# Up products of a SwiGLU block in row halves of the array: two of 64 rows side by side instead of one of 128

## The chip, the core and the metric

The kernel runs on one core of a Trainium2 chip. The metric is the device time of one execution in microseconds (us): 907.65 us is the median of three runs of the kernel before (907.55 to 908.18). The core has a matrix engine (TensorE; PE in the profile, with its weight loads listed apart as PEld), a vector engine (DVE), an activation engine (ACT), GpSimd (POOL) and SyncE (SP), the last two here mainly for starting DMA transfers. TensorE reads both operands from SBUF and writes to PSUM, which here is handed out as four tiles of two banks; one bank holds 512 fp32 values in each of 128 partitions.

## The reference

Hash attention on four batches of eight heads, and then a SwiGLU feed-forward block over all 3,072 rows of its output:

```python
scores = scale * np.matmul(q, k.transpose(0, 1, 3, 2))
scores = np.where(mask, scores, -1000000000.0)       # mask: q and k fall into the same bucket
...
x = attn_out.transpose(0, 2, 1, 3).reshape(B * S, H * D)      # 3072 x 512
g = x @ w_gate                                                # 512 x 1536
silu = g * (1.0 / (1.0 + np.exp(-g)))
val = x @ w_val
return (silu * val @ w_out).astype(np.float32)
```

The change concerns only `x @ w_gate` and `x @ w_val`, the "up" products.

## The kernel before, in words

**Two stages.** Attention comes first (0 to about 314 us of the profile), then the feed-forward block (314 us to the end), in `gated_block`. The order of work on every engine is written out by hand: instructions run on each engine in the order in which the program issues them.

**Split values.** The feed-forward block multiplies in the one-pass fp32 form of TensorE (`FP32R`). For accuracy each operand is kept in three parts: a high part h (index 0), a low part l (index 1) and their difference d (index 2). A product needs one accumulator for h and l together, called `a`, and one for the differences, called `n`. The result is `a` times a constant minus `n`.

**Tiling.** The 3,072 rows of x are taken in three blocks of 1,024 (`WB`), the 1,536 columns of the weights in twelve pieces `f` of 128. x lies transposed, so that its 512 columns are the contraction: four slices j of 128 (`NJ` = 4). For one piece F and one of "gate" and "value", the function `up` makes one up product: 128 columns of the weights by 1,024 rows of x, accumulated over four slices j. PSUM tile `a` gets 16 matrix instructions of 128 contraction rows and 512 columns (4 slices x 2 parts x 2 halves of the 1,024), and tile `n` gets 8 (4 slices x 1 part x 2 halves). The two halves lie in two different banks of the tile. There are 3 x 12 x 2 = 72 up products, so 1,152 instructions into `a` and 576 into `n`.

**Order around them.** In `atoms_of`, an up product has two atoms. The atom `one` issues `first` (all into `a`) and has ACT copy `a` out of PSUM, scaled (line 787). The atom `other` issues `second` (all into `n`); then DVE subtracts `n` (line 794). For the gate, ACT applies Silu (line 796). For the value, DVE multiplies with the gate (line 798), and ACT and DVE split the result into three parts, `hid` (lines 799, 805 and 808). After each three pieces f a "down" product D follows: eight chunks of nine instructions (128 rows, 512 columns) into PSUM tiles `o`, which read `hid` and w_out. In each block the order is U0 to U3, D0, U4 to U6, D1, U7 to U9, D2, U10, U11, D3, where each U is a gate and a value up product. In D3 the first four chunks begin with the two older of their three `hid` pieces, since the third is still being made.

**Row halves elsewhere.** In attention, the score products (line 549, tile `sc`) already use 64 contraction rows each: the head in partitions 0 to 63 writes one bank of its tile and the head in partitions 64 to 127 the other. The products with v (line 580, tile `av`) use 64 output columns, the row sums and hashes (tile `joint`) 32.

**Weights.** Each up product reads one ring tile of 768 KB, brought from DRAM by POOL (`bring`, line 251), six tiles in all. A ring tile comes free when the last instruction of `second` has read it.

Of the kernel before, what the change touches and what calls it, by code (L numbers as in the profile page):

```python
# [19 lines left out]
def kernel(  # L20
# [20 lines left out]
    nc = tc.nc  # L41
# [3 lines left out]
    P = 128  # L45
# [7 lines left out]
    NJ = DM // P  # L53
    NF = DF // P
    PIECE = 512
    NQ = 3
    assert DF % P == 0 and DM == PIECE and NF % NQ == 0
    WB = 2 * PIECE
    NB = B * S // WB
    assert NB * WB == B * S and S < WB < 2 * S and NF // NQ > 2  # L60
    assert 2 * D == P and S == NCH * P and NCH % 2 == 0 and HQ <= 512 and DM <= 512
# [19 lines left out]
    def two_banks(name):  # L81
        return pp.tile([P, 2, 512], FP32, tag="pp", name=name)
# [3 lines left out]
    def r32(t):  # L86
        return t.bitcast(FP32R)
# [8 lines left out]
    for f in range(NF):  # L96
        for src in (moe_w_gate, moe_w_val):
            pieces.append(src.rearrange("(j p) c -> p j c", p=P)[:, :, 2 * f * P : 2 * (f + 1) * P])
        if f % NQ == 0 and f or f == NF - 1:
            done = (f + 1) // NQ * NQ if f == NF - 1 else f  # L100
            for g in range(done - NQ, done):
                pieces.append(moe_w_out[g * P : (g + 1) * P, :])
    place = {}
    n = 0
    for f in range(NF):
        place["g", f], place["v", f] = n, n + 1
        n += 2
        if f % NQ == 0 and f or f == NF - 1:
            done = (f + 1) // NQ * NQ if f == NF - 1 else f
# [3 lines left out]
    NPIECE = len(pieces)  # L113
    ram = [dram.tile([P, 3, PIECE], FP32R, tag=f"ram{i}", name="ram") for i in range(NPIECE)]
    words = {}
# [7 lines left out]
    def load_words(count, queue=None):  # L123
        queue = queue or queues[0]
        for i in range(len(words), min(count, NPIECE)):
            words[i] = t = wordp.tile([P, PIECE, 2], I32, tag="words", name="words")
            to = t.rearrange("p f w -> p (f w)")
# [4 lines left out]
    def scale(i):  # L132
        t = words[i]
        if i // 2 not in stages:
            stages[i // 2] = stagep.tile([P, 2, 3, PIECE], FP32, tag="stage", name="stage")
        staged[i] = st = stages[i // 2][:, i % 2]
# [104 lines left out]
    def bring(count=1):  # L241
        for _ in range(count):
# [6 lines left out]
            pool = ringp[2 <= i % sum(RINGS) < 2 + RINGS[1]]  # L249
            held[what, n] = t = pool.tile([P, 3, PIECE], FP32R, tag="ring", name="ring")  # L250
            nc.gpsimd.dma_start(t.bitcast(FP32), ram[at].bitcast(FP32))  # L251
# [3 lines left out]
    xparts = {}  # L255
# [480 lines left out]
    def gated_block(scope):  # L736
# [2 lines left out]
        hidp = scope.enter_context(tc.tile_pool(name="hidp", bufs=4))  # L739
        outp = scope.enter_context(tc.tile_pool(name="outp", bufs=1))  # L740
        homes.append(outp)
        hids = {}
        accs = {}
        rows = [out[b * S : (b + 1) * S, :].rearrange("(p c) m -> p c m", c=NCH) for b in range(B)]
        NCB = WB // P

        def mm(ps, w, x, start, stop):
            nc.tensor.matmul(ps, w, x, start=start, stop=stop)  # L748

        def up(F, what):  # L750
            b = F // NF
            w = held[what, F]
            a, n_ = two_banks("a"), two_banks("n")

            def block(v, j):
                return w[:, v, j * P : (j + 1) * P]

            def first():
                for j in range(NJ):
                    for v in range(2):  # L760
                        for half in range(WB // PIECE):
                            mm(a[:, half], block(v, j), r32(xparts[b, j][:, half, v]),
                               j == 0 and v == 0, j == NJ - 1 and v == 1)

            def second():
                for j in range(NJ):
                    for half in range(WB // PIECE):
                        mm(n_[:, half], block(2, j), r32(xparts[b, j][:, half, 2]),
                           j == 0, j == NJ - 1)

            return first, second, a, n_

# [3 lines left out]
        def atoms_of(kind, n):  # L776
            if kind == "U":
# [5 lines left out]
                for what, z in (("g", gate), ("v", val)):  # L783
                    def one(what=what, z=z):
                        ops[what] = up(n, what)
                        ops[what][0]()
                        nc.scalar.activation(two(z), ops[what][2], AF.Copy, scale=STEP + 1)  # L787
# [27 lines left out]
            else:  # L815
# [5 lines left out]
                def start(c, js, steps=None):  # L821
                    if c not in tiles:
                        tiles[c] = two_banks("o")
                    t = tiles[c]
                    cols = slice(c * P, (c + 1) * P)
                    def first():
                        for j in js:
                            for v in range(2):
                                mm(t[:, 0], hs[j][:, v, cols], ws[j][:, v],
                                   j == 0 and v == 0, j == NQ - 1 and v == 1)  # L830

                    def second():
                        for j in js:
                            mm(t[:, 1], hs[j][:, 2, cols], ws[j][:, 2], j == 0, j == NQ - 1)

                    for go in steps or ("ba" if final and c >= ahead else "ab"):
                        (first if go == "a" else second)()
# [93 lines left out]
        for kind, n in order:  # L931
            b, f = divmod(n, NF if kind == "U" else NF // NQ)
# [43 lines left out]
    with ExitStack() as scope:  # L976
        gated_block(scope)
# [32 lines left out]
```

## Time and profile before

| what | value |
|---|---|
| median of three runs | 907.65 us |
| the profiled execution, its own time | 908.05 us |
| its span, first to last instruction | 906.3 us |
| TensorE busy | 901.8 us of the span |
| DVE, ACT, POOL busy | 665.4, 450.4, 90.6 us |
| instructions into `a`, `n`, `o` | 1152, 576, 870 |
| their busy time | 273.0, 142.2, 198.2 us |
| granted TensorE clock, mean | 0.999 |

How to read it: the profile lists groups of instructions by source line, engine and tiles, as "out<-in", with the array tile (rows*columns), the shape, the number, the busy time and the mean length of one. A matrix instruction's length includes the time in which its last columns pass through the array, during which the next one already runs, so lengths overlap. What a stream of them costs is read from the distance between starts. Times are microseconds from the start of the span unless marked ns.

### The profile page before, as it was taken

To read this page: it belongs to the slowest core of one execution; us is meant where nothing else is said; L and a number is where in the kernel's file an instruction comes from. 1 tells how busy PE (TensorE), PEld (TensorE's weight loads), DVE (VectorE), ACT (ScalarE), POOL (GpSimd) and SP (SyncE) were. 2 spreads that over 40 slices of the span, in tenths; PEclk is the share of its full clock that TensorE was granted. 3 is DMA by queue.
4 is the path that set the end of the run, shared out by engine and by line. 5 is a ranking of instruction groups with operands and counts; after the bars stand their busy time and mean duration, and the time that the engine had idled before them with its cause. 6 is when DMAs were issued, how large, how long until landed. Compare 5 with 4: busy or idle time off the path is not lost.

```text
span 906.3 us, 12438 instructions
## 1 busy us (share of the span) xinstructions
PE 901.8 (100%) x4801; PEld 638.4 (70%) x4801; DVE 665.4 (73%) x782; ACT 450.4 (50%) x604; POOL 90.6 (10%) x187
## 2 busy tenths in 40 slices
PE   9999999999999999999999999999999999999998
PEld 5444444444444588888888888888888888888887
DVE  6779999999988977688786856464658754474746
ACT  6788988788888654551524233331313243413220
POOL 2001100010001210011000000101000100001000
PEclk9999999999999999999999999999999999999999
DMA  7567888877877799685758563534434642525332
GB/s 181 109 145 183 190 203 194 205 203 230 229 195 213 225 358 375 240 294 170 300 173 296 193 249 105 180 134 172 142 140 150 250 149 98 200 70 209 104 140 93
DMA packets 142266, 174.24 MB, mean 192 GB/s; under 512 B 103200, under 2 KB 113408, under 8 KB 142208
## 3 DMA queue, kind: packets, MB, share of 16 engines
q0 software_dynamic: 22240, 114.83, 35.8%
q1 hardware_dynamic: 118560, 57.43, 24.5%
q10 hardware_dynamic: 1408, 1.20, 0.5%
q8 instruction: 38, 0.62, 0.3%
q14 instruction: 20, 0.16, 0.1%
HBM read 133.17 MB, written 39.42 MB: 190 GB/s over the span
## 4 chain that ended last, share of the span: by engine, by line
PE 99%; DVE 0%; DVEq 0%; issue 0%
PE a L748 29%; PE o L748 21%; PE sc L549 17%; PE n L748 14%; PE av L580 14%; PE joint L621 1%; PE joint L441 1%; PE idle L375 0%; PE tps L483 0%; DVE o L843 0%; DVE o L851 0%; DVE o L886 0%; DVEq L1005 0%; DVE kb L369 0%
## 5 line engine op out<-in xcount | busy, mean ns | idle before, releaser
L748 PE MATMUL a<-xparts,ring 128*128 128x512 f32 x1152 | 273.0, 389 | 0.0
L748 PEld LDWEIGHTS a<-xparts,ring 128*128 128x128 f32 x1152 | 216.2, 188 | 45.4 <-issue 0.6
L748 PE MATMUL o<-ring,hid 128*128 128x512 f32 (+1 forms) x870 | 198.2, 388 | 0.0
L748 PEld LDWEIGHTS o<-ring,hid 128*128 128x128 f32 x870 | 162.9, 188 | 33.6
L559 ACT ACTIVATE A<-sc 128x768 f32<-128x768 f32 x192 | 154.0, 815 | 1.6 <-PE sc L549 0.8
L549 PE MATMUL sc<-qT,kT 64*128 64x384 f32 x768 | 153.0, 483 | 0.0
L748 PE MATMUL n<-xparts,ring 128*128 128x512 f32 x576 | 142.2, 389 | 0.0
L580 PE MATMUL av<-A,vraw 128*64 128x386 f32 (+1 forms) x768 | 127.7, 488 | 0.0
L748 PEld LDWEIGHTS n<-xparts,ring 128*128 128x128 f32 x576 | 108.1, 188 | 22.4
L794 DVE TENSOR_TENSOR v<-v,n 128x1024 f32<-128x1024 f32 x36 | 44.0, 1221 | 97.5 <-PE n L748 97.0
L251 POOL DMA_DIRECT2D ring<-ram x108 | 57.0, 530 | 498.7 <-PE n L748 302.4
L580 PEld LDWEIGHTS av<-A,vraw 128*64 128x64 f32 x768 | 53.7, 136 | 73.3 <-issue 62.6
L787 ACT ACTIVATE g<-a 128x1024 f32<-128x1024 f32 x36 | 37.0, 1027 | 128.0 <-PE a L748 126.9
L549 PEld LDWEIGHTS sc<-qT,kT 64*128 64x128 f32 x768 | 68.8, 187 | 39.8 <-issue 35.3
L799 ACT ACTIVATE hid<-v 128x1024 fp32r<-128x1024 f32 x36 | 38.2, 1062 | 111.9 <-DVE v L798 108.2
L796 ACT ACTIVATE g<-g 128x1024 f32<-128x1024 f32 x36 | 38.2, 1061 | 87.9 <-DVE g L794 87.9
L855 DVE TENSOR_TENSOR o<-o 128x512 f32<-128x512 f32 x92 | 62.9, 687 | 19.0 <-ACT o L849 16.6
L794 DVE TENSOR_TENSOR g<-g,n 128x1024 f32<-128x1024 f32 x36 | 43.8, 1217 | 37.5 <-PE n L748 37.5
L549 PE MATMUL sc<-qb,kb 64*128 64x384 bf16 x384 | 63.5, 323 | 0.0
L603 DVE SCALAR_TENSOR_TENSOR both<-A 128x1536 f32<-128x1536 f32 x32 | 55.5, 1734 | 4.5 <-ACT A L559 3.0
L805 DVE SCALAR_TENSOR_TENSOR hid<-hid,v 128x1024 fp32r<-128x1024 f32 (+1 forms) x39 | 44.5, 1141 | 18.8 <-ACT hid L799 18.8
L607 DVE TENSOR_TENSOR both<-both,A 128x1536 f32<-128x1536 f32 x32 | 55.9, 1748 | 1.7
(88 smaller groups left out, 695.5 us busy)
## 6 DMA issues: line engine op xcount, KB each, us to landing
ring<-ram POOLq DMA_DIRECT2D x108, 768.0 KB, 5.6
ram<-stage POOLq DMA_DIRECT2D x22, 768.0 KB, 4.5
ram<-stage SPq DMA_DIRECT2D x14, 768.0 KB
vraw<-in_v_dram SPq DMA_DIRECT2D x16, 384.0 KB
kraw<-in_k_dram SPq DMA_DIRECT2D x60, 96.0 KB
qraw<-in_q_dram SPq DMA_DIRECT2D x60, 96.0 KB
r<-sums SPq DMA_DIRECT2D x28, 192.0 KB
out_dram<-o SPq DMA_DIRECT2D x10, 512.0 KB
```

Source lines behind the costliest of these rows:

```text
L251: nc.gpsimd.dma_start(t.bitcast(FP32), ram[at].bitcast(FP32))
L549: nc.tensor.matmul(banks_of[u][:, h], x["k", n][rows, ks], x["q", n][rows, qs], start=start, stop=stop)
L559: nc.scalar.activation(weights(u)[:, :, 0:HQ], banks_of.pop(u), AF.Exp, scale=SCALE * (1.0 if units[u][0] else OFF / 2))
L580: nc.tensor.matmul(ps[h * D : (h + 1) * D, 0:width], raws["v", n][:, h, c, :], a[:, h, 0:width], start=c == 0, stop=c == NCH - 1)
L603: nc.vector.scalar_tensor_tensor(out=t, in0=first, scalar=S * EPS / P / 2, in1=now, op0=ALU.add, op1=ALU.add)
L607: nc.vector.tensor_tensor(t, t, now, op=ALU.add)
L748: nc.tensor.matmul(ps, w, x, start=start, stop=stop)
L794: nc.vector.tensor_tensor(two(z), two(z), n_, op=ALU.subtract)
L796: nc.scalar.activation(z, z, AF.Silu)
L799: nc.scalar.activation(h, val, AF.Copy, scale=TOWARD / STEP)
L805: nc.vector.scalar_tensor_tensor(out=l_, in0=h_.bitcast(FP32), scalar=-STEP, in1=v_, op0=ALU.mult, op1=ALU.add)
L855: nc.vector.tensor_tensor(accs[c], accs[c], t[:, 1], op=ALU.subtract)
```

## The change

An up product's 24 instructions of 128 contraction rows become 48 of 64. They are issued in pairs: one takes partitions 0 to 63 of a slice j and a part v and writes one half of the 1,024 columns, and the other takes partitions 64 to 127 and writes the other half, in the other bank. After one pass over all slices each half has had only half of the contraction. A second pass, with `swap` = 1, gives each half the other 64 partitions. The passes follow one another as: `a`, `n`, `a` swapped (all three in `first`), `n` swapped (in `second`). An added helper `after` puts a dependency between the last instruction of a tile's first pass and the first of its second pass, so that TensorE waits there for its own earlier instruction. In the list of each engine's instructions, nothing but TensorE's is different; DVE, ACT, POOL and SP have the same instructions in the same order.

```diff
+    HALF = P // 2
...
+        def after(later, earlier):
+            with tc.tile_pool(name="turn", bufs=1) as pool:
+                tc.add_manual_dep(pool.alloc_inst, earlier.ins.name, sync, reason="turn")
+                tc.add_manual_dep(later.ins, pool.alloc_inst.name, sync, reason="turn")
...
+            def rows_of(out, v, j, half, at, start, stop):
+                rows = slice(at * HALF, (at + 1) * HALF)
+                return mm(out[:, half], w[rows, v, j * P : (j + 1) * P], r32(xparts[b, j][rows, half, v]),
+                   start, stop)
+
+            ends = {}
+
+            def turn_of(out, vs, swap):
+                for j in range(NJ):
+                    for v in vs:
+                        for at in range(2):
+                            first_, last_ = j == 0 and v == vs[0], j == NJ - 1 and v == vs[-1]
+                            i = rows_of(out, v, j, at ^ swap, at, not swap and first_, bool(swap) and last_)
+                            if at == 0 and first_ and swap:
+                                after(i, ends[vs])
+                            if last_:
+                                ends[vs] = i
+
             def first():
-                for j in range(NJ):
-                    for v in range(2):
-                        for half in range(WB // PIECE):
-                            mm(a[:, half], block(v, j), r32(xparts[b, j][:, half, v]),
-                               j == 0 and v == 0, j == NJ - 1 and v == 1)
+                turn_of(a, (0, 1), 0)
+                turn_of(n_, (2,), 0)
+                turn_of(a, (0, 1), 1)
 
             def second():
-                for j in range(NJ):
-                    for half in range(WB // PIECE):
-                        mm(n_[:, half], block(2, j), r32(xparts[b, j][:, half, 2]),
-                           j == 0, j == NJ - 1)
+                turn_of(n_, (2,), 1)
```

More of the change, by code (lines that the diff above doesn't have):

```diff
@@ L741, in gated_block @@
         homes.append(outp)
+        sync = mybir.DependencyInfo(mybir.DependencyClass.Sync, mybir.DependencyReason.DATA)
+        def after(later, earlier):
+            with tc.tile_pool(name="turn", bufs=1) as pool:
+                tc.add_manual_dep(pool.alloc_inst, earlier.ins.name, sync, reason="turn")
+                tc.add_manual_dep(later.ins, pool.alloc_inst.name, sync, reason="turn")
         hids = {}
@@ L747, in mm @@
         def mm(ps, w, x, start, stop):
-            nc.tensor.matmul(ps, w, x, start=start, stop=stop)
+            return nc.tensor.matmul(ps, w, x, start=start, stop=stop)
         def up(F, what):
```

## The prediction, made before the changed kernel was run

> **What bounds the kernel now.** I read the page's busy times and its chain of waits first, then the chain in order of time, then single stretches of TensorE. The chain says that one engine sets the end:
>
> ```profile
> PE 901.8 (100%) x4801; PEld 638.4 (70%) x4801; DVE 665.4 (73%) x782; ACT 450.4 (50%) x604; POOL 90.6 (10%) x187
> ...
> PE 99%; DVE 0%; DVEq 0%; issue 0%
> PE a L748 29%; PE o L748 21%; PE sc L549 17%; PE n L748 14%; PE av L580 14%; PE joint L621 1%; PE joint L441 1%; PE idle L375 0%; PE tps L483 0%; DVE o L843 0%; DVE o L851 0%; DVE o L886 0%; DVEq L1005 0%; DVE kb L369 0%
> ```
>
> TensorE is on the chain for 99%, and the up products (`a` and `n`) are 43% of it. So what the change does to the pace of TensorE counts in full. The chain in order of time (start, us, what) gives that pace:
>
> ```profile
> 597.76 3.63 PE a L748 x16
> 601.39 1.81 PE n L748 x8
> 603.20 16.32 PE o L748 x72
> 619.52 3.63 PE a L748 x16
> ```
>
> One up product takes 3.63 + 1.81 = 5.44 us for 24 instructions: 226.7 ns each. The down product has the same pace (16.32 / 72 = 226.7), and nothing is lost between them. The question is what a pair of 64-row products costs. The page of before has such pairs in the scores (timeline of TensorE: start, us, instruction):
>
> ```profile
> 303.96 0.33 PE L549 MATMUL sc<-qb,kb 64*128 64x384 bf16 x2
> 304.13 0.81 PE L549 MATMUL sc<-qT,kT 64*128 64x384 f32 x4
> 304.77 0.33 PE L549 MATMUL sc<-qb,kb 64*128 64x384 bf16 x2
> 305.03 0.85 PE L621 MATMUL joint<-acc,ones 128*32 128x384 f32 x8
> ```
>
> A bf16 pair is followed by the next product after 0.17 us, and two fp32 pairs take 0.64 us, so 0.32 each. For 384 columns that is one and two passes: the two halves of a pair do run beside each other. The same pattern begins at 296.70 and at 304.77, ten units apart, so one unit of three pairs takes 0.807 us; five passes of 384 columns at 2.4 GHz would take 0.800. So a pair has about 2.3 ns above its columns. The up products have more: 226.7 against 512 / 2.4 = 213.3, which is 13.4. Eleven ns could be won on each of 1,728 pairs if this surplus came from the full array.
>
> The lengths of single products speak on that (shortest / median / longest ns, by tile):
>
> ```profile
> L748 PE MATMUL o<-ring,hid x870: 221/389/398, 358.2 to 902.5; 128*128 128x512 f32 x172, 128*128 128x384 f32 x1, 128*128 128x128 f32 x1
> L549 PEld LDWEIGHTS sc<-qT,kT x768: 182/187/197, 7.2 to 304.1; 64*128 64x128 f32 x192
> L549 PE MATMUL sc<-qb,kb x384: 322/323/334, 10.3 to 304.8; 64*128 64x384 bf16 x192
> ```
>
> **What the Trainium skill says.** "TensorE: Matmul & The Clock Gate", section "Wait — 56ns, not 53.3ns?", gives 2.4 GHz and about 2.5 ns beyond the columns for a matmul, 215.7 ns at 512 columns. The score pairs agree (2.3 ns); the one-pass fp32 products, at 226.7, don't. "TensorEngine Tiling (Array Packing)", section "Key Properties", says that tiles work independently, and that a change of tiling mode drains TensorE. The trace shows both: pairs side by side, and in the lines above 0.26 us from the last bf16 pair (64*128) to the first of `joint` (128*32), where the same pair is otherwise followed after 0.17. A change of mode costs 0.09 us. The first page's section "Back-to-back issue gap" gives about 81 ns for each load and product of 128 columns in a long stream, so some 40 ns per instruction; no stream here is that dense.
>
> **The change part by part.**
>
> *Pace of the pairs.* 24 full products of an up product become 24 pairs. What a pair of one-pass fp32 costs isn't in the trace, so I bound it. Lower end: as in the scores, 213.3 + 2.3 = 215.6 ns, 11.1 less than now: 1,728 x 11.1 ns = -19.2 us. Upper end of what is likely: another 3 ns, +5.2 us; the second of a pair starts some ns after the first, and two streams read at full rate. I take no difference, 226.7. Reason: the surplus looks like a property of the one-pass fp32 stream, not of the full array. The shortest `o` product, with 128 columns, lasted 221 ns, and one with 512 lasted 389: 168 ns for 384 columns, 1.05 cycles a column. Were the surplus a fixed 13 ns for each swap of weights, the short product would have lasted 389 - 160 = 229 ns or more. Columns at 1.05 cycles make 224.0 for 512, and 2.5 on top make 226.5, which is the pace seen. Against the bf16 pair (323 ns for 384 columns, so by one cycle a column 376 for 512 and 216 for 128) the surplus is 13 ns at 512 columns and 5 at 128: it grows with the columns. And the fp32 score passes, which take two cycles a column, have no surplus either. A half-array stream of one-pass fp32 has the same column rate, so I expect it to be held back in the same way.
>
> *Weight loads.* 24 loads become 48, of the same 128 columns (64 rows). In the scores two fp32 loads go in during one bf16 pair of 0.16 us, and the fp32 products after it keep their 482 ns. So two loads lie beside a pair of 0.227 us: 0. Without this cover, two loads one after the other are bounded by the 128-column products at the end, which are load-bound, at some 112 ns each (estimate: 0.8 us busy for six, less the last one's length): 224 ns, still below 227.
>
> *Changes of mode.* Up products now run in 64*128 and down products in 128*128. There are twelve D, each entered from a U, and eleven left for a U: 23 changes of 0.09 us = +2.1 us. On the path in full, since TensorE is the chain. Ends: 0.06 and 0.13 each, so +1.4 to +3.0. The entry from attention is a change of mode already.
>
> *The waits.* Two in each up product: the second pass over `a` waits for the end of its first pass, and so for `n`. Queued behind the waiting instruction are all of TensorE's. But between the two ends lie four pairs of `n` (0.91 us), or eight of `a` (1.81 us), and a product ends 0.39 us after its start. The signal is there 0.5 us or more before it is needed: 0. If that were wrong, 72 x 2 waits at 0.1 us would be 14 us.
>
> *Copies out of PSUM.* `a` is now complete four pairs before the end instead of eight products, 0.91 us instead of 1.81. ACT's copy takes 1.03 us (row L787), after 0.1 us of signalling, so it ends 0.2 us after `n`, where it used to end 0.7 before. DVE's subtraction starts some 0.2 us later. Who waits: the `hid` of D3 is the tightest. In the block that ends at 494 us, D3 starts at 494.21, its first product with the third piece is due 24 x 0.2267 later, at 499.65, its differences at 500.1, and DVE has made them at 499.51 (timeline). The slack of 0.6 us falls to 0.4: 0. PSUM: tile `n` is written eight pairs into an up product, 1.8 us earlier than now, into the tile of two up products ago. From the end of that one's `n` this is still about 7 us; the latest subtraction in the trace ends 4.9 us after it, near 353 us: 0.
>
> *Ring and other queues.* Ring tiles come free at the end of `second` as now, and POOL waits for TensorE there, not for DMA (302.4 us of its idle time). The instructions of DVE, ACT, POOL and SP don't change: 0.
>
> *Sum.* 908.05 (the profiled execution's own time) + 0 + 2.1 = 910.2. The median of the runs stands 0.4 lower, so 909.8 us. The likeliest case's own range, with a pair from 1 ns below to 3 above and the ends of the mode changes, is -0.3 to +8.2 us: 907 to 916.
>
> **The rivals.**
>
> *A, faster.* The surplus belongs to full-array products, as when a swap of weights can't hide, and goes with the halves: -19.2 + 2.1 = -17.1, so 890.6 us. Its place is the 1,728 pairs, its price 11.1 ns each, and it decides from 1.2 ns a pair on, where the mode changes are paid. For it: every tiled form in the trace, on 64 rows or on 64 columns, runs within some 3 ns of its columns. Against it: all those are two-pass fp32 or bf16, so the one-pass form is as good an explanation, and the slope above supports that.
>
> *B, much slower.* TensorE can't be fed: a pair has two loads and two products, four instructions in 227 ns, 57 each. The densest long stretch of the trace is the scores, twelve in 0.807 us, 67 each. If each took 62 ns (the skill's section "Wait — 56ns, not 53.3ns?" names that for a matmul decoded in microcode), a pair would take 248: +21 x 1,728 = +37, so 947 us. Against it: the 40 ns named above. Two streams at full rate that hinder each other's reads would look alike, with another size.
>
> *C, not side by side.* If one-pass products of the two halves ran one after the other, an up product would take twice its time: +392 us. The score pairs speak against it.
>
> **How the numbers follow.** The likeliest case has 0.58, A 0.20, B and its like 0.20, C 0.02. A difference of 0.2% (1.8 us) is about what a measurement of this kernel can tell from none. Of the likeliest case about 0.39 lies above that, since its +2.1 is barely past the bound and can only be eaten by a shorter pair, 0.16 within and 0.03 below. With A at 0.20 below, B and C above: faster 0.23, same 0.16, slower 0.61. The range takes in A, the likeliest case and the smallest members of B: 889 to 917.
>
> **What would show it.** `a` and `n` as 64*128, 2,304 and 1,152 instructions. Each up product 5.44 us long on the chain in order of time if I am right, 5.2 under A, near 5.9 under B. From `n` to `o` and from `o` to `a` one step of about 0.32 us instead of 0.227. No wait of TensorE for itself; DVE's subtraction about 0.3 us after the end of `n` instead of 0.1. I am wrong if the pair's pace differs from 226.7 by more than a nanosecond or two: each is worth 1.7 us.

## The result, and the profile after

The changed kernel takes 917.34 us (median of four runs, 916.11 to 917.79); the kernel before took 907.60 us in the same comparison (907.39 to 908.18). The ratio is 1.0104, with a 95% interval of 1.0087 to 1.0122: slower by 9.7 us. The profiled execution has a span of 916.0 us against 906.3.

The page of the changed kernel, its busy times, its chain of waits and its groups for the products (source line, engine, tile; then the count, the busy time, the mean ns of one, and the engine's idle time before them with what ended it):

```profile
PE 908.7 (99%) x6529; PEld 634.9 (69%) x6529; DVE 665.9 (73%) x782; ACT 451.5 (49%) x604; POOL 91.0 (10%) x187
...
PE 91%; DVE 6%; DMA 1%; ACT 1%; issue 1%; SPq 0%; DVEq 0%; ACTq 0%
...
L756 PE MATMUL a<-xparts,ring 64*128 64x512 f32 x2304 | 286.3, 387 | 0.0
L756 PE MATMUL o<-ring,hid 128*128 128x512 f32 (+1 forms) x870 | 200.6, 390 | 1.1 <-DVE o L876 1.1
L756 PE MATMUL n<-xparts,ring 64*128 64x512 f32 x1152 | 155.2, 387 | 1.7 <-DVE xparts L300 1.7
```

The number of products is what the change says. TensorE used to be 99% of the chain; now DVE and a transfer are on it, and in the feed-forward stage TensorE for the first time waits for DVE, at two places: before `o` and before `n`. The chain in order of time (start, us, what) shows the pace in between:

```profile
605.58 1.81 PE a L756 x16
607.39 0.91 PE n L756 x8
608.30 16.57 PE o L756 x72
624.86 2.05 PE a L756 x16
626.91 0.92 PE n L756 x8
627.83 1.81 PE a L756 x16
```

A pass of eight pairs into `a` takes 1.81 us and one of four pairs into `n` 0.91, twice each: 5.44 us for an up product, to the hundredth what it was. A pair costs 226.7 ns, so the two halves do run side by side, and nothing is gained by it. What is new stands at the ends: the down product takes 16.57 us instead of 16.32, and the pass after it 2.05 instead of 1.81. That is 0.25 and 0.24 us a change of tiling mode (from full products to row halves or back).

The same timeline shows what `n` waits for at the start of the second block. TensorE first, then DVE (start, us, instruction, count, and in brackets the idle time before it and what ended it):

```profile
513.59 2.12 PE L756 MATMUL a<-xparts,ring 64*128 64x512 f32 x16
515.54 0.63 PE L756 MATMUL n<-xparts,ring 64*128 64x512 f32 x4
516.37 0.51 PE L756 MATMUL n<-xparts,ring 64*128 64x512 f32 x2 [0.19 <-DVE xparts L300]
517.50 0.51 PE L756 MATMUL n<-xparts,ring 64*128 64x512 f32 x2 [0.63 <-DVE xparts L300]
517.84 0.86 PE L756 MATMUL a<-xparts,ring 64*128 64x512 f32 x6
```

```profile
513.77 0.68 DVE L872 SCALAR_TENSOR_TENSOR o<-o 128x512 f32<-128x512 f32 x1
514.49 0.69 DVE L876 TENSOR_TENSOR o<-o 128x512 f32<-128x512 f32 x1
515.09 2.35 DVE L300 TENSOR_TENSOR xparts<-xparts 128x1024 fp32r<-128x1024 f32 x2
```

Two pairs of `n` (slices 0 and 1) run; the third should follow at 516.0 and starts at 516.37, and the fourth comes 1.13 us after the third. They read the difference parts of the new block's x for slices 2 and 3, which DVE makes only now, from 515.09 to 517.4. The kernel before made them equally late after its down product (512.29 to 514.64, where that ended at 510.6), but its `n` began 3.6 us after the down product, not 1.95. Counted as steps beyond 226.7 ns, start to start of a pair, this wait is 1.4 us here (the longer step right after it included), and 1.4 again at the third block: 2.8.

The third place is the first down product, D0. It takes 18.4 us from its first start to its last end, where the others take 16.6. On the chain stands a transfer that DVE, which works in order, waits for before it gets to D0's copies. DVE's timeline, first of the changed kernel, then of the kernel before:

```profile
349.98 1.02 DVE L653 SCALAR_TENSOR_TENSOR last<-last,e,o 128x768 f32<-128x768 f32 x1 [5.12 <-DMA o<-sums]
```

```profile
348.41 1.02 DVE L652 SCALAR_TENSOR_TENSOR last<-last,e,o 128x768 f32<-128x768 f32 x1 [3.14 <-DMA o<-sums]
```

This is the normalisation of attention's last pair of heads. It needs the row sums' reciprocals, broadcast through DRAM.

In sum, in this execution: 12 x 0.25 + 11 x 0.24 = 5.6 us for the changes of mode, 2.8 at the block starts and 1.8 in D0, together 10.2. The feed-forward stage, from the first product into `a` to the end of the span, grew from 591.8 to 602.0 us, by 10.2; attention happened to be 0.5 us shorter.

### The profile page after: what moved, and what is told of

It reads as the page before. It is cut to its first block, busy times and chain, and to the rows that moved or that the text cites. A ratio compares the mean times of both kernels' runs of the same rounds, so it can differ in the third digit from the quotient of the medians.

```text
span 916.0 us, 15894 instructions
## 1 busy us (share of the span) xinstructions
PE 908.7 (99%) x6529; PEld 634.9 (69%) x6529; DVE 665.9 (73%) x782; ACT 451.5 (49%) x604; POOL 91.0 (10%) x187
## 4 chain that ended last, share of the span: by engine, by line
PE 91%; DVE 6%; DMA 1%; ACT 1%; issue 1%; SPq 0%; DVEq 0%; ACTq 0%
PE a L756 27%; PE sc L550 17%; PE o L756 17%; PE av L581 14%; PE n L756 13%; PE joint L622 1%; PE joint L442 1%; DMA o<-sums 1%; DVE o L876 1%; DVE o L872 1%; DVE xparts L300 1%; DVE hid L826 1%; DVE v L819 1%; DVE v L815 1%; DVE xparts L295 1%
## 5 line engine op out<-in xcount | busy, mean ns | idle before, releaser
L756 PE MATMUL a<-xparts,ring 64*128 64x512 f32 x2304 | 286.3, 387 | 0.0
L756 PEld LDWEIGHTS a<-xparts,ring 64*128 64x128 f32 x2304 | 214.9, 184 | 49.2 <-issue 3.8
L756 PE MATMUL o<-ring,hid 128*128 128x512 f32 (+1 forms) x870 | 200.6, 390 | 1.1 <-DVE o L876 1.1
L756 PE MATMUL n<-xparts,ring 64*128 64x512 f32 x1152 | 155.2, 387 | 1.7 <-DVE xparts L300 1.7
L756 PEld LDWEIGHTS n<-xparts,ring 64*128 64x128 f32 x1152 | 107.9, 184 | 25.9 <-DVE xparts L300 3.2
L550 PEld LDWEIGHTS sc<-qT,kT 64*128 64x128 f32 x768 | 68.8, 187 | 39.8 <-issue 35.1
L820 ACT ACTIVATE hid<-v 128x1024 fp32r<-128x1024 f32 x36 | 38.2, 1062 | 89.8 <-DVE v L819 86.8
L817 ACT ACTIVATE g<-g 128x1024 f32<-128x1024 f32 x36 | 38.2, 1061 | 61.8 <-DVE g L815 61.8
L808 ACT ACTIVATE v<-a 128x1024 f32<-128x1024 f32 x36 | 36.9, 1026 | 44.1 <-PE a L756 44.1
```

The lines of the kernel that those rows point to most:

```text
L550: nc.tensor.matmul(banks_of[u][:, h], x["k", n][rows, ks], x["q", n][rows, qs], start=start, stop=stop)
L756: return nc.tensor.matmul(ps, w, x, start=start, stop=stop)
L817: nc.scalar.activation(z, z, AF.Silu)
L820: nc.scalar.activation(h, val, AF.Copy, scale=TOWARD / STEP)
```

## The experiments

Each experiment was compared with the kernel before on its own chip; that kernel's medians lay between 907.47 and 907.86 us. A gain such as "-2.5 us" is counted from the changed kernel's 917.34. Of each kernel one execution was traced, so what is read from a trace holds for that execution, which can differ from the median by up to 3 us (`e7_bring_later`).

### Is it the order or the halves?

`e1_order` keeps full products, in the changed kernel's order of tiles; the numbers are the slices j:

```diff
+            def first():
+                of_a((0, 1))
+                of_n((0, 1))
+                of_a((2, 3))
...
+                of_n((2, 3))
```

> The kernel before, with full 128-row products and no change of tiling mode in the feed-forward stage, but issued in the changed kernel's order: half of the products into a, half of those into n, the rest of a, the rest of n. Theory 'due times': the earlier n and the later end of a cost by themselves what the changed kernel's trace shows, 2.8 us at the starts of the second and third block (TensorE waits for DVE's difference parts of x) and 1.8 us in the first down product, so +4.6 us, about 912.2 us, with both waits in the trace. Rival 'half array': the loss comes from half-array products and the changes of mode alone, so 907.6 us and no waits.

Measured: 907.75 us, ratio 1.0007 (0.9998 to 1.0015), no waits in the feed-forward stage; D0 took 16.5 us. The rival's number came out, but the test was built badly: with the slices split, `n` needs slices 2 and 3, whose parts are late, only at its end. What it does show is that a later end of `a` costs nothing, at D0 either. `e5_col_halves` mends it: full products, one half of the columns after the other (the numbers are now the halves), so that `n` needs all four slices as early as in the changed kernel.

```diff
+            def first():
+                of_a(0)
+                of_n(0)
+                of_a(1)
...
+                of_n(1)
```

> The kernel before, with full 128-row products, issued half of the columns after half: a for columns 0 to 511 over all four slices, n for them, a for the other columns, n for them. Unlike in e1_order, every slice's difference part is needed as early as in the changed kernel. Theory 'due times': the waits of n for DVE's x parts at the starts of the second and third block come back, 1.4 us each, and nothing else: +2.8 us, 910.3 us. Rival: only half-array products wait there: 907.5 us.

Measured: 911.72 us, ratio 1.0046 (1.003 to 1.0063), +3.9 us. TensorE's waits (in total, how often, the longest):

```profile
PE n L748 <- DVE xparts L299: 2.5, 4, 0.6
PE idle L375 <- DVE kb L369: 1.0, 1, 1.0
PE o L748 <- DVE o L860: 0.4, 1, 0.4
```

The waits for x are back without a single half-array product: 1.8 us at each of the two block starts in steps beyond 226.7 ns, 3.6 in all. They are a matter of due times. Another 0.7 us is D0 again (17.2 us), to which I come below. In this trace the stage grew by 4.6 us, and attention was 0.7 us shorter than in that of the kernel before, hence the 3.9.

### What does a change of mode cost?

`e6_modes` is the kernel before with the last slice of `n` in 64-row pairs; nothing else moves:

```diff
+                for again in range(2):
+                    for at in range(2):
+                        part = slice(at * (P // 2), (at + 1) * (P // 2))
+                        mm(n_[:, at], w[part, 2, (NJ - 1) * P : NJ * P],
+                           r32(xparts[b, NJ - 1][part, at, 2]), False, again == 1)
```

> The kernel before, with the last slice of n in each up product as two pairs of 64-row products instead of two full ones (the same pair twice, so that half of that slice's sum is left out and the other half counted twice): 144 changes of mode, no other work moved. Theory 'a change costs its second product too', 0.21 us: +30 us, 938 us. Rival 'first step only', 0.09 us: +13 us, 920.5 us.

Measured: 938.91 us, ratio 1.0345 (1.033 to 1.0361), 31.1 us more: 0.216 us a change. Its chain has the same number:

```profile
601.14 3.86 PE a L748 x16
605.00 2.02 PE n L748 x10
607.02 3.86 PE a L748 x16
```

An up product with two changes takes 3.86 + 2.02 = 5.88 us, 0.44 more than 5.44. Start to start, the first product behind a change comes 318 to 326 ns after its predecessor, and the next again 335 to 339 ns, instead of 227 each: the change is paid twice. In the changed kernel, with its long stretches, these two steps (318 and 335) make 0.20 us, and nine more steps of 224 to 236 ns the rest of the 0.25; here the second change comes before that tail has run out. The second step isn't special to a change of mode: in the changed kernel it also follows the waits for DVE (335 to 342 ns behind the four at which the stream starts up again).

`e2_one_mode` takes the changes out of the changed kernel instead, by making the down products in row halves too:

```diff
+                    def some(vs):
+                        for j in js:
+                            for v in vs:
+                                done[c] = done.get(c, 0) + 1
+                                for at in range(2):
+                                    rows_ = slice(at * HALF, (at + 1) * HALF)
+                                    mm(t[:, at], hs[j][rows_, v, cols], ws[j][rows_, v],
+                                       done[c] == 1, done[c] == 3 * NQ)
```

> The changed kernel, with the down products in row halves too (rows 0 to 63 into one bank, rows 64 to 127 into the other, so that a chunk's two banks no longer hold its two sums; number and size of the work are the same): 22 of 23 changes of mode go. Theory 'a change costs its second product too', about 0.21 us each: -4.6 us, 912.7 us. Rival 'a change costs only the first step', 0.09 us as the prediction had it: -2.0 us, 915.3 us. The waits for x at the block starts stay in both.

Measured: 914.82 us, -2.5 us, between the two. Its trace says why: the twelve down products but the first and the last take 16.5 us as before, so the changes are gone, but the waits have grown. D0 takes 19.6 us instead of 18.4 (16.5 without waits now), `n` waits once more ahead of it (0.5), and the block starts wait 3.6 us instead of 2.8, together some 2.7 us. 22 changes at some 0.24 us less 2.7 make -2.6. As a test of the price alone it was poor, since time that TensorE saves just ahead of a wait is waited.

### The waits

`e3_early_x` has DVE make the next block's x parts earlier in the last down product of a block:

```diff
-                    if at in (7, 10):
+                    if at in (6, 8):
```

> The changed kernel, with DVE's low and difference parts of the next block's x issued one and two chunks earlier in the last down product of a block. Theory 'due times': the two waits of n (1.37 and 1.43 us) go, -2.8 us, 914.5 us. Rival: DVE is late as a whole there and the wait moves to the copies out of PSUM, no gain, 917.3 us.

Measured: 915.27 us, -2.1 us. The waits for x are gone, but part of them came back under another name: `n` now waits for DVE's copies of `o` (0.69 and 0.78 us, counted as before), so 1.3 of the 2.8 us are won; D0 was 0.7 us shorter in this run.

`e4_first_full` leaves the up products ahead of D0 as they were:

```diff
+                if F < 4:
+                    ...
+                    return
```

> The changed kernel, with the first four pieces' up products (block 0, before the first down product) as in the kernel before. Theory 'late a': the first down product's waits for DVE (1.8 us) come from the later copy of a in the busiest stretch of ACT and DVE and go, with one change of mode (0.2 us): -2.0 us, 915.3 us. Rival: DVE is late there for other reasons: -0.2 us, 917.1 us, and the first down product still lasts 18.4 us.

Measured: 915.86 us, -1.5 us; D0 takes 16.5 us and has no wait, as the theory said. Its reason, a late `a`, was wrong all the same: `e1_order` has the same late `a` and no wait. DVE's timeline had pointed at the broadcast. `e7_bring_later` was to move two of the large ring loads that are issued just ahead of that broadcast away from it:

```diff
-                    if count[0] == 4:
+                    if count[0] == 11:
                         bring(2)
```

> The changed kernel, with the two ring loads of block 0 that are issued beside the last pair's row sums moved seven atoms later. Theory 'DMA': the first down product is late because DVE, in order, stands before the last pair's normalisation, whose broadcast lands behind the bulk loads; it lands earlier, and the first down product takes 16.6 us instead of 18.4: -1.8 us, 915.5 us. Rival 'late a' (later copies of a by ACT): still 18.4 us, 917.3 us.

Measured: 916.39 us (915.85 to 919.36), the same as the changed kernel. But the edit moved nothing. The loads (POOL) and the broadcast (SPq), first in the timeline of the changed kernel, then in that of `e7_bring_later`:

```profile
337.03 1.57 POOL L252 DMA_DIRECT2D ring<-ram  x3 [11.00 <-DMA xram<-late]
338.62 1.35 SPq L646 DMA_DIRECT2D o<-sums  x2
```

```profile
337.60 1.57 POOL L252 DMA_DIRECT2D ring<-ram  x3 [11.22 <-DMA xram<-late]
339.11 1.35 SPq L646 DMA_DIRECT2D o<-sums  x2
```

The three loads still go out just ahead of the broadcast. Ring loads are issued in one fixed order, each when its tile is free, whichever call asks for them, and every engine does the changed kernel's work in the changed kernel's order. So whether the loads delay the broadcast stays untested, and the run is a second measurement of the changed kernel. As such it is of use: in its traced execution, the slowest of the four, D0 took 19.5 us instead of 18.4 and DVE waited 6.42 us for the broadcast instead of 5.12, and the medians of one and the same work lie 0.95 us apart. A difference of a microsecond between two of these kernels says little by itself, and a single trace's D0 can't be taken for its kernel's. What the traces together show is how D0 follows the broadcast (the time is from the start of TensorE's last row-sum instruction to that of DVE's normalisation; `e6_modes` and `e9_fp32`, which reach D0 later, are left out):

| kernel | up products ahead of D0 | normalisation after, us | D0, us |
|---|---|---|---|
| e10_combined | full | 33.3 | 16.5 |
| e4_first_full | full | 33.7 | 16.5 |
| e1_order | full | 34.2 | 16.5 |
| before | full | 34.3 | 16.5 |
| e11_two_full | half of them full | 34.4 | 16.6 |
| e5_col_halves | full | 35.1 | 17.2 |
| e12_rest | full | 35.4 | 17.4 |
| e3_early_x | halves | 35.7 | 17.7 |
| e8_bf16 (below) | full, bf16 | 36.0 | 19.3 |
| after | halves | 36.4 | 18.4 |
| e7_bring_later | halves | 37.7 | 19.5 |
| e2_one_mode | halves | 38.2 | 19.6 |

Up to 34.4 us D0 waits for nothing, and beyond it loses nearly what the broadcast is late (`e8_bf16` more, since it reaches D0 1.2 us sooner). The kernel before stands right at that edge. In the four traces with row halves there, it came 1.4 to 3.9 us later than before. One thing that sets these four apart is a 16 KB transfer of instructions, 19 us after the last row sums: TensorE uses up instructions twice as fast. `e11_two_full` moves it, with `F < 2` in place of `F < 4` above:

> The changed kernel, with only the first two pieces' up products (the first 21.8 us of the feed-forward stage) as before, so that TensorE's instructions are fetched as seldom there, and row halves run while the last pair's broadcast is under way. Theory 'fetch': in all four kernels with row halves in these pieces a 16 KB instruction transfer falls 19 us after the last row sum, just ahead of the last pair's small transfers, and they land late (DVE's normalisation 35.7 to 38.2 us after it, instead of 33.3 to 35.1); without it DVE starts by 34.5 us and the first down product takes 16.6 us. Rival 'row halves slow the transfers': DVE starts after 35.7 us again, and the first down product takes 17.7 us or more.

Measured: 916.30 us, -1.0 us, no more than the spread above. Its instruction transfer came at 30.2 us instead of 19, DVE started 34.4 us after the row sums, and D0 took 16.6. That fits the transfer, and speaks against row halves as such slowing the broadcast. But `e12_rest`, with no transfer there, had 35.4, and `e8_bf16`, with neither a transfer nor row halves there, 36.0, while the changed kernel's work gave 36.4 once and 37.7 another time. So this landing scatters by more than a microsecond anyway, and the cause of its lateness isn't settled.

### The parts together

`e10_combined` joins `F < 4` with still earlier x parts, `at in (4, 6)`:

> The changed kernel, with the first four pieces' up products as before and the next block's low and difference parts of x issued three and four chunks earlier. Theory: the waits of n for x (2.8 us) and those of the first down product (1.8 us) go, and one change of mode; what stays above the kernel before is 22 changes at 0.21 us, so 912.2 us. Rival (there is a loss of the half-array products themselves, or the early x makes the copies out of PSUM late): 914 us or more.

Measured: 917.29 us, no gain at all. D0 has no wait, but x came too early: the last down product of the first two blocks takes 18.9 us, and TensorE waits there for the copies of `o`:

```profile
PE o L756 <- DVE o L889: 3.3, 4, 1.1
PE idle L376 <- DVE kb L370: 1.0, 1, 1.0
```

In both attempts DVE had no room at the end of a block: its work can be shifted, and the wait moves along. `e12_rest` joins `F < 4` with the milder `at in (6, 8)`:

> The changed kernel, with the first four pieces' up products as before and the next block's low and difference parts of x one and two chunks earlier (as in e3_early_x). Theory: 22 changes of mode at 0.21 us (4.7 us) and what e3_early_x left of the waits at the block starts (1.3 us) stand above the kernel before: 913.5 us. Rival: another loss of the row halves appears: 915 us or more.

Measured: 914.76 us, ratio 1.0076 (1.0061 to 1.0091), 6.9 us above the kernel before. In its trace, of the slowest of its four executions, the stage is 7.9 us longer than in that of the kernel before. The waits make 0.69 and 0.81 us at the block starts and 0.9 in D0, which was late after all; 22 changes at 0.245, the changed kernel's price, make 5.4. Together that is 7.8 us, and next to nothing is left to explain.

### Where do 226.7 ns come from?

`e8_bf16` makes the products into `a` from a constant bf16 tile, full array, a weight load for each (one run):

```diff
-                            mm(a[:, half], block(v, j), r32(xparts[b, j][:, half, v]),
+                            mm(a[:, half], flat[:, 0:P], flat,
```

> The kernel before, with the 1,152 products into a made from a constant bf16 tile in place of x and the weights (the output has no gate or value sum), in the full array, each with its own weight load. Theory 'one-pass fp32 stream': they follow one another every 215.7 ns, an up product takes 5.27 us, about 895 us in all. Rival 'full array': 226.7 ns as before, 907.5 us.

Measured: 900.78 us. Lengths of that kernel's instructions into `a` (shortest, median, longest ns), and two pieces of its chain:

```profile
L751 PE MATMUL a<-flat x1116: 379/379/390, 314.2 to 876.6; 128*128 128x512 bf16 x186
```

```profile
584.54 3.47 PE a L751 x16
588.01 1.84 PE n L751 x8
```

A bf16 product lasts 379 ns instead of 389, and the most frequent step from one to the next is 216 ns. An up product takes 5.31 us. The total is higher than expected because the one-pass `n` beside it runs at 230 ns, for a reason that no run shows, and because D0, reached earlier, waited (19.3 us). `e9_fp32` puts the products into `n` in the multi-pass form (one run):

```diff
-                        mm(n_[:, half], block(2, j), r32(xparts[b, j][:, half, 2]),
+                        mm(n_[:, half], block(2, j).bitcast(FP32), xparts[b, j][:, half, 2],
```

> The kernel before, with the 576 products into n in the multi-pass fp32 form instead of the one-pass form, in the full array, with the same operands. In the scores this form makes two instructions of two cycles a column. Theory 'one-pass fp32 stream': at two cycles a column the surplus is gone, 426.7 + 2.5 = 429 ns an instruction, +364 us in all. Rival 'surplus of the full array and its fp32 weight loads': 440 ns, +377 us.

Measured: 1272.15 us, +364.5. Its chain:

```profile
604.72 3.64 PE a L748 x16
608.36 6.87 PE n L748 x16
```

Eight products have become sixteen instructions; in 6.87 us they are 429 ns each, two cycles a column and some 2.5 ns. So the full array, with a weight load for each product, costs 216 ns in bf16 and 429 in multi-pass fp32, next to nothing above the columns. Only the one-pass fp32 stream has the surplus, and row halves don't take it away. One rival isn't excluded by these two runs alone: an fp32 weight load that gets in the way of a product only when that is short. A load lasts 188 ns in the kernel before, but 98 in `e8_bf16`, and in `e9_fp32` 190 beside instructions twice as long. Against it stand the last products of the kernel before, one-pass ones of 128 columns: each has a full fp32 load, and they follow each other every 111 ns.

## Why the prediction was wrong

The forecast was 909.8 us, slower, in a range of 889 to 917; 917.34 came. Its direction was right, and so was the likeliest case, but only as to the pace. Step by step:

**Pace of the pairs: right.** No difference was taken, 226.7 ns; 226.7 it is. The reason given, that the surplus belongs to the one-pass fp32 stream, is borne out by `e8_bf16` and `e9_fp32`. With that rival A falls, and with the pace B and C do.

**Weight loads: right.** 24 more loads in each up product cost nothing.

**Changes of mode: right in kind, too small by more than half.** "23 changes of 0.09 us = +2.1 us", with an upper end of 0.13, against 0.216 in `e6_modes` and 0.24 in the changed kernel's chain: 5.0 to 5.6 us. The price was taken from the first step behind a change alone, in the attention stage, where the products that follow were not looked at. That first step came as forecast, 318 ns; what was missing is the second (335) and the tail behind it, more than half of the price. The kernel before held the whole price, in its chain at the one change that leads into the feed-forward stage:

```profile
314.57 3.87 PE a L748 x16
318.45 1.81 PE n L748 x8
320.26 1.81 PE a L748 x8
```

Here the first up product's `a` takes 3.87 us, and every other takes 3.63: 0.24 us. The Trainium skill's sentence that a change of mode drains TensorE ("TensorEngine Tiling (Array Packing)", section "Key Properties") agrees with the runs, in which the stream behind a change starts as it does behind a wait (335 ns and 335 to 342 in the second step), but it gives no price; one stretch with a change set against one without is the way to get it.

**The waits of TensorE for itself: right.** None is listed in the changed kernel.

**Copies out of PSUM: right as far as it went, but the step that was missing belongs here.** DVE's subtraction did come later, and neither the third `hid` piece nor tile `n` was late. But the prediction asked only who waits for what `n` writes into, and when `n` is complete. It did not ask whether what `n` reads is there 1.7 us sooner. The difference parts of the next block's x were not, at two block starts: 2.8 us, put at 0. `e5_col_halves` shows that this needs no row halves, and `e3_early_x` that the lateness of those parts causes it.

**Ring and other queues: "The instructions of DVE, ACT, POOL and SP don't change: 0".** Their order didn't change, but a broadcast that they wait for landed about 2 us later in the traced execution, at a place with no slack in the kernel before: 1.8 us in D0, put at 0. D0's dependence on the landing is shown; why it landed later is open, and part of it may be scatter.

**The range.** Its upper end rested on a longer pair and 0.13 us for a change. With 0.24 for a change and the two waits, the prediction's own sum would have been 908.05 + 10.2 = 918.3, less 0.4 for the median: 917.9, past the upper end.

## What to carry to other kernels

Side-by-side row tiles won nothing here, where the full array already streamed at the pace of its data type; find out first to what a surplus per product belongs, by the pace of another type in the same array. A change of tiling mode between two long streams cost 0.22 to 0.25 us here, seen in the pieces that follow it, not in the first step. When a product moves ahead, check that its inputs are ready at the new time as well as where its output goes.

## What the runs showed of the hardware that I hadn't expected

One-pass fp32 products of 512 columns follow each other every 226.7 ns in the full array and in 64-row pairs alike, while bf16 in the full array takes 216 and each instruction of multi-pass fp32 429.

A change of mode lengthens two steps, not one: 227 ns become some 318 and then some 335, and nine more are a few ns longer. The step of 335 to 342 ns also follows when TensorE starts up again after a wait.

TensorE's instruction stream is fetched in transfers of 16 KB, which the profile lists as a queue of their own: 38 of them for the 9,602 products and weight loads of the kernel before, and 51 for the 13,058 of the changed one.
